# Loading the V weights and computing the first V product in column halves, the normalisations of later chunks one step sooner, and more filler before one double visit, in a fused attention and gated-MLP kernel

## The chip, the cores and the metric

The kernel runs on one core of one Trainium2 chip. The metric is device microseconds of one execution, given as a median of several runs. The profile's span is about 1.7 us shorter than the device time of the same run (263.7 against 265.41 us before the change).

Names used below: PE is TensorE's matmul row and PEld its weight loads, DVE is VectorE, ACT is ScalarE, POOL is GpSimd, SP the engine that issues the transfers. PSUM is the memory that matmuls write; this kernel uses eight banks of it.

## The reference

The result is `x + attention(norm(x)) + mlp(norm(x))` for 2048 rows of 512 columns in bf16:

```python
xn = _layernorm(x, axis=-1)
# attention: 32 heads of 16 columns, each query sees itself and the 255 keys before it
q, k, v = split(xn @ wqkv)
p = softmax(where(mask, q k^T / 4, -1e9));  a = (p @ v) @ wo
# MLP without a nonlinearity, F = 1792
m = ((xn @ w_gate) * (xn @ w_up)) @ w_down
return x + a + m
```

## The kernel before

The rows are handled in four chunks T of 512 (four blocks b of 128 rows each). The heart is a list of 75 *score steps*. A step computes a PSUM tile of scores (there is only one such tile, four banks), ACT takes its exponential, POOL and DVE mask it. Between steps PE is filled from a list of other matmuls ("fillers": gate, up, down, Q/K/V products), in amounts set by a small cost model on the host: `GAP` is the least amount of filler after a step and `SHIFT` moves filler between steps. After some steps the *value sums* of one group of heads (a single visit) or of two groups (a double visit) are computed.

```python
GAP = 9.6
PAIRS = ((0,), (1,), (2,), (3,)), ((0, 1), (2, 3)), ((0, 1), (2, 3)), ((0, 1), (2,))   # visits of each chunk
SHIFT = {20: -2, ..., 62: 3, 63: 6, 64: 8, 66: 8, 67: 6, 68: 4, 69: 2}

# loads, all from SP in this order
for lo, hi in ((0, 1), (1, 2), (2, 4)):                      # x, blocks 0, 1, 2-3
    nc.sync.dma_start(out=self.x[:, lo:hi, :], in_=xv[:, lo:hi, :])
for lo in (1024, 512, 0):                                    # V, K, Q weights, 512 KB each
    nc.sync.dma_start(out=self.Wqkv[:, :, lo:lo + 512], in_=wq[:, :, lo:lo + 512])
# ... cut: the other weights and the rest of x

# the first chunk: DVE normalises, PE transposes (ACT copies the transpose out), PE makes V
self.norm_transpose(0, False)
self.keep_busy(8)                                            # eight idle matmuls
for b in range(4):
    if b < 3:
        self.norm_transpose(b + 1, False)
    self.proj_v(b, engine="act" if b == 2 else "dve")
    if b == 0:
        self.norm_apply(3)
self.proj_qk(0, 0, 1, engine="dve")                          # K, then Q, then the first score step

# the normalisations of chunk T+1 run beside five score steps of chunk T
for i, fs in norms(T + 1, 0, 1).items():
    self.beside[self.first[T, 0] + (5, 6, 7, 8, 9)[i]] = fs

# a normalisation: DVE statistics, POOL scale (rs), then DVE applies it
nc.vector.tensor_scalar(out=xn[:], in0=self.x[:, t, :], scalar1=mv[:, j, 0:1],
                        scalar2=rs[:, j:j + 1], op0=ALU.subtract, op1=ALU.mult)

# a finished output block leaves its PSUM bank through DVE
nc.vector.tensor_tensor(out=y, in0=ps, in1=y, op=ALU.add)

# a visit of the value sums takes two PSUM banks for each group of heads
accs = [self.ps_m.tile([128, 512], F32, tag="M", name="acc") for _ in range(2)]
```

The softmax here doesn't subtract the row's maximum and nothing guards it: scores larger than these inputs give would overflow.

Of the kernel before, what the change touches and what calls it, by code (L numbers as in the profile page):

```python
# [22 lines left out]
REST = (((0, *SIX), (1, *SIX), (0, *FOUR)), ((1, *FOUR), (2, *FOUR)), ((2, *SIX), (3, *SIX), (3, *FOUR)))  # L23
SCORES, VALUES, SECOND = 1.9, 6.0, 5.0
FIRST = 3
GAP = 9.6
PAIRS = ((0,), (1,), (2,), (3,)), ((0, 1), (2, 3)), ((0, 1), (2, 3)), ((0, 1), (2,))
SHIFT = {20: -2, 21: -5, 22: -8, 23: -11, 24: -14, 26: -10, 27: -7, 28: -3, 62: 3, 63: 6, 64: 8, 66: 8, 67: 6, 68: 4, 69: 2}
MASKED, FIRST_DIVIDE, SECOND_DIVIDE = 8, 8, 24
COPY = dict(act=2.8, dve=3.2)  # L30
EXP, MASK, HALF, SUMS, DIVIDE, TURN, STATS = 8.7, 1.9, 1.7, 4.2, 8.2, 6.1, 4.2
# [2 lines left out]
class Kernel:  # L34
# [26 lines left out]
    def setup(self):  # L61
        nc, const, NT, NF = self.nc, self.const, self.NT, self.NF
        self.x = const.tile([128, NT, 512], BF16, name="x")
        self.Wqkv = const.tile([128, 4, 1536], BF16, name="Wqkv")
        self.Wo = const.tile([128, 4, 512], BF16, name="Wo")
        self.Wg = const.tile([128, 4, self.F], BF16, name="Wg")
        self.Wu = const.tile([128, 4, self.F], BF16, name="Wu")
        self.Wd = const.tile([128, NF, 512], BF16, name="Wd")
        xv = self.x_d.rearrange("(t p) d -> p t d", p=128)
        wq = self.w_d["qkv"].rearrange("(k p) n -> p k n", p=128)  # L70
        wg = self.w_d["g"].rearrange("(k p) n -> p k n", p=128)
        wu = self.w_d["u"].rearrange("(k p) n -> p k n", p=128)
        for lo, hi in ((0, 1), (1, 2), (2, 4)):
            nc.sync.dma_start(out=self.x[:, lo:hi, :], in_=xv[:, lo:hi, :])
        for lo in (1024, 512, 0):
            nc.sync.dma_start(out=self.Wqkv[:, :, lo:lo + 512], in_=wq[:, :, lo:lo + 512])
        h = self.F // 2
        for lo in (0, h):
            nc.sync.dma_start(out=self.Wg[:, :, lo:lo + h], in_=wg[:, :, lo:lo + h])
            nc.sync.dma_start(out=self.Wu[:, :, lo:lo + h], in_=wu[:, :, lo:lo + h])  # L80
            if lo == 0:
                nc.sync.dma_start(out=self.x[:, 4:8, :], in_=xv[:, 4:8, :])
        nc.sync.dma_start(out=self.Wd[:], in_=self.w_d["d"].rearrange("(f p) n -> p f n", p=128))
        wo = self.w_d["o"].rearrange("(c p) n -> p c n", p=128)
        for c in range(4):
            nc.sync.dma_start(out=self.Wo[:, c, :], in_=wo[:, c, :])
        for lo, hi in ((8, 10), (10, 12), (12, NT)):
            nc.sync.dma_start(out=self.x[:, lo:hi, :], in_=xv[:, lo:hi, :])

        warm = const.tile([128, 1], F32, name="warm")  # L90
        nc.vector.memset(warm[:], 0.0)
        nc.scalar.activation(out=warm[:], in_=warm[:], func=ACT.Exp)
        self.idle = const.tile([128, 128], BF16, name="idle")
        nc.vector.memset(self.idle[:], 0.0)
        self.keep_busy(40)
        ident = const.tile([128, 128], BF16, name="ident")
        nc.gpsimd.memset(ident[:], 0.0)
        nc.gpsimd.affine_select(out=ident[:], in_=ident[:], compare_op=ALU.not_equal, fill=1.0,
                                base=0, pattern=[[-1, 128]], channel_multiplier=1)
        self.ident = ident  # L100
        pi = const.tile([128, 1], I32, name="pi")
        nc.gpsimd.iota(pi[:], pattern=[[0, 1]], base=0, channel_multiplier=1)
        podd = const.tile([128, 1], I32, name="podd")
        nc.vector.tensor_scalar(out=podd[:], in0=pi[:], scalar1=4, scalar2=1,
                                op0=ALU.arith_shift_right, op1=ALU.bitwise_and)
        self.odd = const.tile([128, 1], F32, name="odd")
        nc.vector.tensor_copy(out=self.odd[:], in_=podd[:])
        self.mhalf = const.tile([128, 4], F32, name="mhalf")
        nc.gpsimd.memset(self.mhalf[:], -0.5)
        self.diag = const.tile([128, 64], BF16, name="diag")  # L110
        self.far = const.tile([128, 64], BF16, name="far")
        nc.gpsimd.memset(self.diag[:], BIG)
        nc.gpsimd.memset(self.far[:], BIG)
        for half in (slice(0, 64), slice(64, 128)):
            self.triangle(self.diag[half], True)
            self.triangle(self.far[half], False)
        self.xnT, self.Q, self.hT, self.OT = {}, {}, {}, {}
        self.K, self.Ko, self.V, self.VS = {}, {}, {}, {}
        self.strips, self.parts, self.at = {}, {}, {}
        self.stock = []  # L120
        self.new_values()
# [109 lines left out]
        else:  # L231
            nc.vector.tensor_copy(out=out, in_=in_)

    def proj_v(self, t, ks=range(4), engine=None):
        nc = self.nc
        T, b = divmod(t, 4)
        ps = self.bank(ks, "vp")
        for k in ks:
            nc.tensor.matmul(ps[:], lhsT=self.xnT[T][:, b, k, :],  # L239
                             rhs=self.Wqkv[:, k, 1024:1536], start=(k == 0), stop=(k == 3))  # L240
        if 3 not in ks:
            return
        self.copy(self.heads(self.V[T])[:, b].rearrange("p (r g) d -> p r g d", r=2)[:, :, :, 0:16],
                  ps.rearrange("p (g r d) -> p r g d", g=16, r=2), engine)
# [21 lines left out]
    def first_chunk(self):  # L266

        self.new_chunk(0)
        for b in range(2):
            self.norm_stats(b, 1)  # L270
            self.norm_scale(b, 1)
        for b in (0, 1, 2):
            self.norm_apply(b)
            if b < 2:
                self.norm_stats(b + 2, 1)
                self.norm_scale(b + 2, 1)
        self.norm_transpose(0, False)
        self.keep_busy(8)
        for b in range(4):
            if b < 3:  # L280
                self.norm_transpose(b + 1, False)
            self.proj_v(b, engine="act" if b == 2 else "dve")
            if b == 0:
                self.norm_apply(3)
        self.proj_qk(0, 0, 1, engine="dve")
        self.proj_qk(0, 0, 0, engine="act")
        self.swap_halves(0, self.nc.scalar)
        self.proj_qk(0, 1, 1, engine="dve")
# [160 lines left out]
    def fillers(self):  # L449


        out = []
# [21 lines left out]
        def gu(T, fs, between={}):  # L474
            for f in fs:
                for ks in halves:
                    add(2, lambda f=f, ks=ks: self.gate(T, f, ks))
                for ks in halves:
                    add(2, lambda f=f, ks=ks: self.up(T, f, ks))
                for g in between.get(f, ()):  # L480
                    add(*g)

        def norms(T, at, step):

            t, out = 4 * T, {}
            for b in range(4):
                for k, f in enumerate((lambda b=b: self.norm_stats(t + b, 1),
                                       lambda b=b: self.norm_scale(t + b, 1),
                                       lambda b=b: self.norm_apply(t + b),
                                       lambda b=b: self.norm_transpose(t + b, True))):  # L490
                    out.setdefault(at + step * b + (0, 0, 1, 1)[k], []).append((0, f))
            return out

        def down(T, b, part=range(0, NF, 2)):
            for lo in part:
                add(1.5 if (T, b) == (NCH - 1, 3) else 2, lambda lo=lo: self.down(T, b, lo, lo + 2))

        def wo(T, b, cs):
            add(len(cs), lambda: self.wo(T, b, cs), None, self.last[T, cs[-1]])
# [4 lines left out]
        for T in range(NCH):  # L504
            if T:
                if T + 1 < NCH:
                    for i, fs in norms(T + 1, 0, 1).items():
                        self.beside[self.first[T, 0] + (5, 6, 7, 8, 9)[i]] = fs
                gu(T, range(FIRST))
                for b in range(4):  # L510
                    down(T - 1, b)
                    wo(T - 1, b, range(4))
                    add(0, lambda T=T, b=b: self.store(T - 1, b))
                gu(T, range(FIRST, NF))
            else:
                gu(T, range(NF), norms(1, 1, 3))
            if T + 1 < NCH:
                project(T + 1)
        T = NCH - 1
# [6 lines left out]
    def run(self):  # L526
# [47 lines left out]
        for g, s in enumerate(steps):  # L574
# [8 lines left out]
            self.scores(*s)  # L583
            upto = max(total * (g + 1) / len(steps) + SHIFT.get(g, 0), spent + GAP)
            if g in (1, 2):
# [80 lines left out]
```

## Time and profile before

| | before |
|---|---|
| device time, median of the first 3 runs | 265.57 us |
| span of the profile | 263.7 us |
| PE busy | 98% |
| first score step starts | 13.53 us |
| the five double visits | 2.56, 2.40, 2.60, 2.40, 2.57 us |

From the page of the kernel before: the span, the busy time of the engines, and the engines on the chain that ended last.

```profile
span 263.7 us, 8896 instructions
...
PE 259.6 (98%) x3890; PEld 120.3 (46%) x3890; DVE 174.2 (66%) x341; ACT 175.9 (67%) x142; POOL 117.3 (44%) x278
...
PE 97%; DVE 1%; DMA 1%; issue 0%
```

The list of waits of PE (engine, line, what it waited for, us in total, times, longest) names only the start:

```profile
PE wps L127 <- DVE idle L94: 1.1, 1, 1.1
PE xTp L209 <- DVE xn L190: 0.3, 1, 0.3
```

The chain that ended last lists the value sums with start and length. These are the five double visits of the kernel before:

```profile
89.78 2.56 PE acc L366 x190
...
124.48 2.40 PE acc L366 x175
...
155.57 2.60 PE acc L366 x162
...
187.72 2.40 PE acc L366 x175
...
221.40 2.57 PE acc L366 x177
```

The start, as PE saw it (start, length, engine, line, operation; in brackets the idle time before and what ended it; wps are idle matmuls, xTp transposes, vp V products, S scores):

```profile
5.14 0.40 PE L209 MATMUL xTp<-ident,xn 128*128 128x128 bf16 x4
5.37 0.61 PE L127 MATMUL wps<-idle 128*128 128x128 bf16 x8
6.32 0.40 PE L209 MATMUL xTp<-ident,xn 128*128 128x128 bf16 x4 [0.34 <-DVE xn L190]
6.75 1.02 PE L239 MATMUL vp<-Wqkv,xnT 128*128 128x512 bf16 x4
...
9.12 1.89 PE L239 MATMUL vp<-Wqkv,xnT 128*128 128x512 bf16 x8
...
13.53 0.28 PE L312 MATMUL S<-Q,K 16*64 16x192 bf16 x4
```

The V weights were complete at 6.62 us (the last of the 16 completion records of that transfer), so the first V product at 6.75 could not have come much sooner.

### The profile page before, as it was taken

What the parts mean: (1) busy time and instruction counts of PE and PEld (TensorE: products, weight loads), DVE (VectorE), ACT (ScalarE), POOL (GpSimd) and SP (SyncE); (2) the same over time, 40 slices, a digit from 0 to 9 for tenths busy, and PEclk for the clock granted to TensorE, in tenths of its full rate; (3) what the DMA queues carried; (4) which work ended last, traced back from release to release, by engine and by line L of the source; (5) the groups of instructions that cost most, each with busy time, mean ns of one, the idle gap of its engine ahead of it and who ended that gap; (6) DMA issues with size and microseconds to landing.
All of it is one profiled execution on the core that took longest, in us unless ns stands there. A gap on an engine that the chain in (4) does not pass through costs nothing.

```text
span 263.7 us, 8896 instructions
## 1 busy us (share of the span) xinstructions
PE 259.6 (98%) x3890; PEld 120.3 (46%) x3890; DVE 174.2 (66%) x341; ACT 175.9 (67%) x142; POOL 117.3 (44%) x278
## 2 busy tenths in 40 slices
PE   7999999999999999999999999999999999999995
PEld 7444444444444544444544454444544445444453
DVE  6677888777726697557963679766685235887244
ACT  3467688888757776677775567767777546887500
POOL 6225343325447744333455654544453452554600
PEclk9999999999999999999999999999999999999999
DMA  6999911220002710002000320001100100000002
GB/s 206 374 354 341 268 21 22 24 47 4 0 22 54 69 24 0 4 0 47 5 0 22 81 65 2 0 2 24 27 4 0 42 21 25 2 0 2 4 2 80
DMA packets 19431, 15.12 MB, mean 57 GB/s; under 512 B 7360, under 2 KB 19392, under 8 KB 19392
## 3 DMA queue, kind: packets, MB, share of 16 engines
q1 hardware_dynamic: 18848, 14.26, 20.3%
q8 instruction: 30, 0.49, 0.8%
q10 hardware_dynamic: 544, 0.30, 0.4%
q14 instruction: 9, 0.07, 0.1%
HBM read 9.70 MB, written 2.10 MB: 45 GB/s over the span
## 4 chain that ended last, share of the span: by engine, by line
PE 97%; DVE 1%; DMA 1%; issue 0%
PE gp L395 19%; PE up L406 19%; PE psd L428 17%; PE qkp L251 11%; PE S L312 10%; PE acc L366 7%; PE vp L239 5%; PE psd L434 5%; PE L L428 2%; DMA x<-in_A_x_dram 1%; DVE st L169 1%; PE L L434 1%; PE L L366 0%; PE xTp L209 0%; DVE xn L190 0%; DVE mv L170 0%
## 5 line engine op out<-in xcount | busy, mean ns | idle before, releaser
L319 ACT ACTIVATE P<-S 128x2048 bf16<-128x2048 f32 x75 | 140.7, 1876 | 51.5 <-PE S L312 44.6
L158 POOL TENSOR_SCALAR_AFFINE_SELECT P<-P 64x256 bf16<-64x256 bf16 x224 | 101.3, 452 | 126.0 <-ACT P L319 111.6
L395 PE MATMUL gp<-xnT,Wg 128*128 128x512 bf16 x224 | 60.2, 380 | 0.0
L406 PE MATMUL up<-xnT,Wu 128*128 128x512 bf16 x224 | 58.8, 380 | 0.0
L411 DVE TENSOR_TENSOR hT<-up,gsb 128x512 bf16<-128x512 f32 x56 | 38.3, 684 | 18.6 <-PE up L406 11.6
L428 PE MATMUL psd<-Wd,hT 128*128 128x512 bf16 (+1 forms) x210 | 48.0, 369 | 0.0
L343 DVE TENSOR_TENSOR P<-P,diag 128x512 bf16<-128x512 bf16 (+1 forms) x75 | 29.1, 388 | 9.5 <-ACT P L319 9.5
L428 PEld LDWEIGHTS <-hT 128*128 128x128 bf16 x238 | 21.3, 98 | 25.1 <-issue 2.9
L406 PEld LDWEIGHTS <-Wu 128*128 128x128 bf16 x224 | 20.6, 98 | 25.6 <-issue 2.3
L395 PEld LDWEIGHTS <-Wg 128*128 128x128 bf16 x224 | 20.1, 98 | 24.9 <-issue 2.1
L312 PE MATMUL S<-Q,K 16*64 16x320 bf16 (+4 forms) x720 | 31.0, 260 | 0.0
L312 PE MATMUL S<-Q,Ko 32*64 32x320 bf16 (+4 forms) x720 | 31.0, 260 | 0.0
L251 PE MATMUL qkp<-xnT,Wqkv 128*128 128x512 bf16 x128 | 29.9, 380 | 0.0
L230 ACT ACTIVATE gsb<-gp 128x512 bf16<-128x512 f32 x40 | 23.5, 596 | 7.5 <-PE gp L395 6.7
L312 PEld LDWEIGHTS <-K 16*64 16x64 bf16 x720 | 12.1, 103 | 30.7 <-issue 30.7
L372 DVE STREAM_TRANSPOSE at<-acc 128x512 f32<-128x512 f32 x30 | 19.3, 690 | 6.8 <-PE acc L366 6.8
L444 DVE TENSOR_TENSOR x<-psd,x 128x512 bf16<-128x512 f32 (+1 forms) x15 | 9.7, 653 | 16.4 <-PE psd L434 16.4
L251 PEld LDWEIGHTS <-Wqkv 128*128 128x128 bf16 x128 | 11.7, 98 | 14.5 <-issue 1.6
L366 PE MATMUL acc<-P,V 64*32 64x320 bf16 (+4 forms) x672 | 18.0, 253 | 0.0
L366 PE MATMUL acc<-P,VS 64*32 64x320 bf16 (+4 forms) x672 | 18.0, 253 | 0.0
L366 PEld LDWEIGHTS <-V 64*32 64x32 bf16 x720 | 15.0, 91 | 2.4 <-issue 2.0
L239 PE MATMUL vp<-Wqkv,xnT 128*128 128x512 bf16 x64 | 15.3, 380 | 0.0
(54 smaller groups left out, 198.2 us busy)
## 6 DMA issues: line engine op xcount, KB each, us to landing
out_dram<-x SPq DMA_DIRECT2D x15, 128.0 KB, 1.7
Wg<-in_B_w_gate_dram SPq DMA_DIRECT2D x2, 896.0 KB, 10.9
Wu<-in_B_w_up_dram SPq DMA_DIRECT2D x2, 896.0 KB, 12.5
Wd<-in_B_w_down_dram SPq DMA_DIRECT2D x1, 1792.0 KB, 17.6
Wqkv<-in_A_wqkv_dram SPq DMA_DIRECT2D x3, 512.0 KB, 5.4
x<-in_A_x_dram SPq DMA_DIRECT2D x2, 512.0 KB, 8.3
VS<-V SPq DMA_DIRECT2D x6, 144.0 KB, 2.6
x<-in_A_x_dram SPq DMA_DIRECT2D x3, 256.0 KB, 7.1
```

Of the source, the lines that this page charges most:

```text
L158: nc.gpsimd.affine_select(out=v, in_=v, pattern=pattern + [[1 if diag else -1, 64]], compare_op=ALU.is_ge if diag else ALU.is_gt, fill=0.0 ...
L230: nc.scalar.activation(out=out, in_=in_, func=ACT.Copy)
L239: nc.tensor.matmul(ps[:], lhsT=self.xnT[T][:, b, k, :], rhs=self.Wqkv[:, k, 1024:1536], start=(k == 0), stop=(k == 3))
L251: nc.tensor.matmul(ps[:], lhsT=self.Wqkv[:, k, lo:lo + 128], rhs=self.xnT[T][:, :, k, :], start=(k == 0), stop=(k == 3))
L312: nc.tensor.matmul(S[64 * par:64 * par + 64, e, col:col + n], lhsT=(self.Ko if par else self.K)[U, c][rows, keys], rhs=self.Q[T, c][rows, ...
L319: nc.scalar.activation(out=P[:, :, 0:col], in_=S[:, :, 0:col], func=ACT.Exp, scale=0.25)
L343: self.nc.vector.tensor_tensor(out=v, in0=v, op=ALU.min, in1=self.diag.unsqueeze(1).unsqueeze(1).to_broadcast([128, 4, n, 64]))
L366: nc.tensor.matmul(accs[par][32 * e:32 * e + 32, q:q + n], lhsT=v, rhs=P[rows, e, col:col + n], start=(i == 0), stop=(i == len(todo) - 1), ...
L395: nc.tensor.matmul(ps[:], lhsT=self.Wg[:, k, 128 * f:128 * f + 128], rhs=self.xnT[T][:, :, k, :], start=(k == 0), stop=(k == 3))
L406: nc.tensor.matmul(ps[:], lhsT=self.Wu[:, k, 128 * f:128 * f + 128], rhs=self.xnT[T][:, :, k, :], start=(k == 0), stop=(k == 3))
L411: nc.vector.tensor_tensor(out=self.hT[T, f][:], in0=ps[:], in1=self.gsb[:], op=ALU.mult)
L428: nc.tensor.matmul(ps, lhsT=self.hT[T, f][:, 128 * b:128 * b + 128], rhs=self.Wd[:, f, c0:c1], start=(f == 0), stop=False)
```

## The change

Four edits with one intent, to take small waits of PE away: V weights in two column halves so that half of the first V product can fill the wait at 6.0 us; the second half after the transposes of block 1; the normalisations of later chunks one score step sooner; and more filler before the fifth double visit (`GAP`, `SHIFT`). The late loads of x are merged from three to two.

```diff
-GAP = 9.6
+GAP = 10.6
-SHIFT = {..., 62: 3, 63: 6, 64: 8, 66: 8, 67: 6, 68: 4, 69: 2}
+SHIFT = {..., 62: 3, 63: 6, 64: 12, 66: 12, 67: 11, 68: 9, 69: 6, 70: 3}
-        for lo in (1024, 512, 0):
-            nc.sync.dma_start(out=self.Wqkv[:, :, lo:lo + 512], in_=wq[:, :, lo:lo + 512])
+        for lo, hi in ((1024, 1280), (1280, 1536), (512, 1024), (0, 512)):
+            nc.sync.dma_start(out=self.Wqkv[:, :, lo:hi], in_=wq[:, :, lo:hi])
-        for lo, hi in ((8, 10), (10, 12), (12, NT)):
+        for lo, hi in ((8, 12), (12, NT)):
# cut: proj_v takes cols=(lo, hi), multiplies those columns, and copies out when hi is 512
-        self.keep_busy(8)
-        for b in range(4):
-            if b < 3:
-                self.norm_transpose(b + 1, False)
-            self.proj_v(b, engine="act" if b == 2 else "dve")
-            if b == 0:
-                self.norm_apply(3)
+        self.keep_busy(4)
+        self.proj_v(0, cols=(0, 256))
+        first = self.cur
+        self.norm_transpose(1, False)
+        self.cur = first
+        self.proj_v(0, engine="act", cols=(256, 512))
+        self.norm_apply(3)
+        self.proj_v(1, (0, 1))
+        self.norm_transpose(2, False)
+        self.proj_v(1, (2, 3), engine="dve")
+        self.norm_transpose(3, False)
+        self.proj_v(2, engine="act")
+        self.proj_v(3, engine="dve")
-                        self.beside[self.first[T, 0] + (5, 6, 7, 8, 9)[i]] = fs
+                        self.beside[self.first[T, 0] + (4, 5, 6, 7, 8)[i]] = fs
```

In PE's order the start differs as written; of the steps, only 64 to 72 differ (22 matmuls instead of 18 before the fifth double visit, then +2, -2, -2, -2).

More of the change, by code (lines that the diff above doesn't have):

```diff
@@ L25 @@
 FIRST = 3
-GAP = 9.6
+GAP = 10.6
 PAIRS = ((0,), (1,), (2,), (3,)), ((0, 1), (2, 3)), ((0, 1), (2, 3)), ((0, 1), (2,))
-SHIFT = {20: -2, 21: -5, 22: -8, 23: -11, 24: -14, 26: -10, 27: -7, 28: -3, 62: 3, 63: 6, 64: 8, 66: 8, 67: 6, 68: 4, 69: 2}
+SHIFT = {20: -2, 21: -5, 22: -8, 23: -11, 24: -14, 26: -10, 27: -7, 28: -3, 62: 3, 63: 6, 64: 12, 66: 12, 67: 11, 68: 9, 69: 6, 70: 3}
 MASKED, FIRST_DIVIDE, SECOND_DIVIDE = 8, 8, 24
@@ L232, in copy, with proj_v @@
             nc.vector.tensor_copy(out=out, in_=in_)
-    def proj_v(self, t, ks=range(4), engine=None):
+    def proj_v(self, t, ks=range(4), engine=None, cols=(0, 512)):
         nc = self.nc
         T, b = divmod(t, 4)
-        ps = self.bank(ks, "vp")
+        lo, hi = cols
+        ps = self.bank(ks if lo == 0 else (), "vp")
         for k in ks:
-            nc.tensor.matmul(ps[:], lhsT=self.xnT[T][:, b, k, :],
-                             rhs=self.Wqkv[:, k, 1024:1536], start=(k == 0), stop=(k == 3))
-        if 3 not in ks:
+            nc.tensor.matmul(ps[:, lo:hi], lhsT=self.xnT[T][:, b, k, :],
+                             rhs=self.Wqkv[:, k, 1024 + lo:1024 + hi], start=(k == 0), stop=(k == 3))
+        if 3 not in ks or hi < 512:
             return
```

## The prediction

> **What bounds the kernel now.** TensorE (PE). The page gives PE 98% busy; the chain that ended last is 97% PE, and the waits show PE idle only twice: 1.1 us before its first matmul and 0.3 us at 6.0 us (for the second normalised block). From 13.5 us on, PE's timeline is one packed sequence: a score step costs about 0.36 us, a 512-column matmul 0.215 us, a double visit of the value sums 2.40 to 2.60 us, wherever they stand. Reordering after 13.5 us cannot shorten that sum. Slack is left only in the start (V products end at 11.0 us), about 0.04 us in the third double visit (2.60 us against its siblings' 2.56), and the tail of stores, which is not touched.
>
> **What the change does, costed.**
> 1. Start. Four idle matmuls (0.06 us each) go; the first V product becomes 4+4 matmuls of 256 columns (0.87 us in all, as before), one half before and one after the transposes of block 1. Old timeline: block-0 transposes 5.14, xnT copies on ACT 5.46 to 6.12, V weights landed 6.62 (DMA completions), second xn 6.26, V products from 6.75 to 11.0. New: half the V weights should land near 6.0 (estimate: 512 B packets at about 27 ns, between 18 ns for 256 B and 36 ns for 768 B). Half product 6.05 to 6.5, transposes of block 1 at 6.5 (0.2 us LATER than before, as PE is in order), other half 6.9 to 7.3, V(1) from 7.55 when its 0.60 us ACT copy is done, transposes of block 2 at 8.0, of block 3 at 8.7 (before 8.88: no DVE copy stands before xn(3) now), V(2) at 9.1, V(3) ends near 10.8. Gain about 0.2 us; nothing if the half weights land 0.25 us later; best case 0.35.
> 2. Norms a step sooner: DVE and DMA work off the critical path, at most 0.04 us.
> 3. GAP and SHIFT: the built order differs only in steps 64 to 72: 22 matmuls instead of 18 before the fifth double visit, then +2, -2, -2, -2. The sum is unchanged: no gain. Steps 69 to 72 become about 2.62 us long. There is one score tile: a step lasts at least the 0.50 us until exp starts plus its 1.88 us, about 2.45 us (estimate from these); ten-matmul steps of 2.62 us ran before without a stall.
> 4. V weights in two transfers: K weights land about 0.25 us later than 8.1 us, Q at about 9.9; both are needed after 10.8.
>
> The Trainium skill, "TensorE: Matmul & The Clock Gate", section "What's actually happening", says the array runs at half clock until it was busy for a window of about 3.4 us. The trace agrees: the clock turns full at 4.69 us, 3.6 us after the first idle matmul. Fewer idle matmuls after that do not bring it back; the gaps stay under 0.5 us.
>
> **Prediction.** 265.57 to about 265.38 us; 8 in 10 between 264.95 and 265.70. Faster by over 2%: 0.01; within 2%: 0.98; slower by over 2%: 0.01.
>
> **What would show it.** Start: first Q/K matmul at about 10.8 us instead of 11.0, first score at 13.3 instead of 13.53, every later score shifted alike until step 64. Step 3: no new PE wait between steps 64 and 73, the tail from the last value visit still 11.5 us. Wrong: transposes of block 1 after 6.7 us, or PE waiting for ACT before V(1) and V(2) for over 0.4 us in all.
>
> **What would make it wrong.** Slower 512 B packets; a PSUM or ACT stall in steps 69 to 72 (up to 0.5 us slower); a larger gain if the first half lands before the xnT copies.

## More of the kernel before

A double visit needs all four remaining PSUM banks at once.

The waits of PEld in a window around the first double visit (89 to 93 us), cut to the line that matters:

```profile
PEld L366 <- DVE x L444: 0.2, 1, 0.2
```

DVE around the first visit (start, length, engine, line, operation; in brackets the idle time before and what ended it):

```profile
88.19 0.39 DVE L343 TENSOR_TENSOR P<-P,diag 128x512 bf16<-128x512 bf16 x1
89.85 0.48 DVE L190 TENSOR_SCALAR xn<-x,mv,rs 128x512 bf16<-128x512 bf16 x1 [1.27 <-POOL rs L182]
90.25 0.67 DVE L444 TENSOR_TENSOR x<-psd,x 128x512 bf16<-128x512 f32 x1
```

DVE stood idle for 1.27 us until POOL delivered `rs` for a normalisation, and only then did it take the next instruction in its order, which empties the PSUM bank `psd`. That ended at 90.92 us. The visit began at 89.70, and its third bank was that one: the first weight load of the second group of heads is recorded at 90.982 us, 0.20 us after the instruction before it. The wait of the third visit stands earlier, before the ninth instruction of the visit (155.73 us), and the trace puts it down to another DVE instruction that follows the same kind of normalisation: the copy of a gate product (L232), which also empties a PSUM bank.

## The result

The changed kernel took 265.14 us (median of 6 runs, 264.93 to 265.49) against 265.46 us (6 runs, 265.25 to 265.64). The ratio is 0.9991 with a 95% interval of 0.9978 to 1.0003. A ratio here is the mean time of one kernel's fast runs over that of the other's of the same rounds, so it is not quite the ratio of the medians. Two later sets of the same kernel gave 0.9976 (0.9964 to 0.9988) and 0.9975 (0.9962 to 0.9988). So it is faster by 0.2 to 0.7 us, far inside 2%.

The profile of the changed kernel has the same span as before, 263.7 us (its run, 265.40 us, was one of the slower of the six), but not for want of differences. Two large ones cancel. First, the five double visits, again from the chain that ended last:

```profile
90.28 2.40 PE acc L373 x175
...
124.82 2.40 PE acc L373 x175
...
155.91 2.40 PE acc L373 x175
...
187.86 2.40 PE acc L373 x175
...
222.41 2.40 PE acc L373 x175
```

All five take 2.40 us now; 0.16, 0.20 and 0.17 us are gone. DVE around the first of them:

```profile
87.47 0.48 DVE L190 TENSOR_SCALAR xn<-x,mv,rs 128x512 bf16<-128x512 bf16 x1 [1.27 <-POOL rs L182]
87.88 0.41 DVE L350 TENSOR_TENSOR P<-P,diag 128x512 bf16<-128x512 bf16 x1
89.09 0.69 DVE L451 TENSOR_TENSOR x<-psd,x 128x512 bf16<-128x512 f32 x1 [0.81 <-PE psd L441]
```

The same wait of 1.27 us for POOL is still there, but a step earlier, and the bank is emptied at 89.78 us, as soon as PE has finished with it and before the visit begins at 90.20.

Second, the start. The waits of PE:

```profile
PE wps L127 <- DVE idle L94: 1.1, 1, 1.1
PE vp L240 <- DMA Wqkv<-in_A_wqkv_dram: 0.7, 1, 0.7
```

and its timeline:

```profile
5.36 0.40 PE L209 MATMUL xTp<-ident,xn 128*128 128x128 bf16 x4
5.59 0.39 PE L127 MATMUL wps<-idle 128*128 128x128 bf16 x4
6.12 0.67 PE L240 MATMUL vp<-Wqkv,xnT 128*128 128x256 bf16 x4
6.62 0.39 PE L209 MATMUL xTp<-ident,xn 128*128 128x128 bf16 x4
7.66 1.03 PE L240 MATMUL vp<-Wqkv,xnT 128*128 128x256 bf16 x6 [0.65 <-DMA Wqkv<-in_A_wqkv_dram]
...
9.61 1.90 PE L240 MATMUL vp<-Wqkv,xnT 128*128 128x512 bf16 x8
...
14.03 0.28 PE L319 MATMUL S<-Q,K 16*64 16x192 bf16 x4
```

The first half product filled the gap as intended (6.12 us), but the second half of the weights was complete only at 7.62 us, a whole microsecond after the old single transfer. PE waited 0.65 us for it, and the first score step came at 14.03 us instead of 13.53.

So the first profile suggested a theory that is not the predicted one. **Theory B**: the gain comes from the double visits, mostly through the sooner normalisations, and the new start costs time. The rivals: **theory A**, the prediction (start gains, the rest is nothing), and **chance**: the late weights, or the wait in the fifth visit, are accidents of one execution.

### The profile page after: what moved, and what is told of

The parts are those of the page before. It is cut to its first block, busy times and chain, and to the rows that moved or that the text cites. A ratio compares the mean times of both kernels' runs of the same rounds, so it can differ in the third digit from the quotient of the medians.

```text
span 263.7 us, 8896 instructions
## 1 busy us (share of the span) xinstructions
PE 259.1 (98%) x3890; PEld 120.7 (46%) x3890; DVE 174.7 (66%) x341; ACT 176.1 (67%) x142; POOL 116.9 (44%) x278
## 4 chain that ended last, share of the span: by engine, by line
PE 96%; DMA 2%; SPq 1%; issue 0%; DVE 0%
PE gp L402 19%; PE up L413 19%; PE psd L435 17%; PE qkp L252 11%; PE S L319 10%; PE acc L373 6%; PE vp L240 5%; PE psd L441 5%; PE L L435 2%; DMA Wqkv<-in_A_wqkv_dram 2%; PE L L441 1%; PE L L373 0%; SPq L74 0%; SPq L76 0%; PE xTp L209 0%
## 5 line engine op out<-in xcount | busy, mean ns | idle before, releaser
L230 ACT ACTIVATE gsb<-gp 128x512 bf16<-128x512 f32 x39 | 22.9, 596 | 8.2 <-PE gp L402 7.4
L240 PE MATMUL vp<-Wqkv,xnT 128*128 128x512 bf16 (+1 forms) x68 | 15.6, 367 | 0.8 <-DMA Wqkv<-in_A_wqkv_dram 0.7
```

What stands on the lines that cost most here:

```text
L230: nc.scalar.activation(out=out, in_=in_, func=ACT.Copy)
L240: nc.tensor.matmul(ps[:, lo:hi], lhsT=self.xnT[T][:, b, k, :], rhs=self.Wqkv[:, k, 1024 + lo:1024 + hi], start=(k == 0), stop=(k == 3))
```

## The experiments

Twelve runs were made, four in each of three sets (two of them repeat the changed kernel unaltered, one repeats e4_old_start); the kernels of a set ran on one chip beside the kernel before. All gave correct results. "Visits" are the lengths of the double visits from start to start in PE's timeline; "first score" is the start of the first score step.

| run | what it is | median us | ratio to before (95%) | first score | visits 1, 3, 5 |
|---|---|---|---|---|---|
| before (first profile) | | 265.46 to 265.69 | 1 | 13.53 | 2.56, 2.60, 2.57 |
| e1_norms | norms only | 265.12 | 0.9980 (0.9966 to 0.9993) | 13.35 | 2.40, 2.40, 2.81 |
| e2_shift | GAP, SHIFT only | 265.64 | 1.0000 (0.9988 to 1.0013) | 13.59 | 2.82, 2.80, 2.40 |
| e3_start | start only | 265.92 | 1.0010 (0.9998 to 1.0023) | 13.94 | 2.83, 2.79, 2.40 |
| e4_old_start | all but the start | 264.83 | 0.9969 (0.9957 to 0.9982) | 13.42 | 2.40, 2.40, 2.40 |
| after_again | changed kernel | 264.88 | 0.9976 (0.9964 to 0.9988) | 13.73 | 2.40, 2.40, 2.40 |
| e5_halves_in_order_only | changed, V weights whole | 265.55 | 0.9999 (0.9987 to 1.0011) | 13.84 | 2.40, 2.40, 2.40 |
| e6_halves_in_load_only | e4, V weights in halves | 265.21 | 0.9993 (0.9973 to 1.0014) | 14.69 | 2.40, 2.40, 2.40 |
| e7_stream_place | e1, four idle matmuls fewer | 265.66 | 1.0001 (0.9989 to 1.0013) | 13.87 | 2.40, 2.40, 2.42 |
| e8_k_halves | e4, V weights in row halves | 265.29 | 0.9979 (0.9967 to 0.9992) | 14.67 | 2.40, 2.40, 2.40 |
| e9_old_start_again | e4 repeated | 265.04 | 0.9970 (0.9958 to 0.9982) | 13.48 | 2.40, 2.40, 2.40 |
| after_third | changed kernel | 265.04 | 0.9975 (0.9962 to 0.9988) | 13.72 | 2.40, 2.40, 2.40 |
| e10_old_shift | changed, old GAP, SHIFT | 265.22 | 0.9979 (0.9967 to 0.9991) | 13.85 | 2.40, 2.40, 2.40 |

The two columns on the right account for nearly everything. Take from each profile's span the start of the first score step and what the double visits took over 2.40 us: 249.62 to 249.76 us are left in thirteen of the fourteen profiles (249.64 before, 249.66 after). The fourteenth, e5, has 250.26, with a wait of 0.5 us told below. So little room is left for any other effect of the change on the profiled executions, the merged late loads of x included, which no run tests alone.

### Each part alone, and all but the start

**e1_norms**, the kernel before with one line changed:

```diff
-self.beside[self.first[T, 0] + (5, 6, 7, 8, 9)[i]] = fs
+self.beside[self.first[T, 0] + (4, 5, 6, 7, 8)[i]] = fs
```

> Kernel before with only the norms a step sooner. Theory A (as predicted): they are off the critical path, at most 0.04 us faster. Theory B (from the two traces): in the first and third double visit TensorE waits 0.16 and 0.20 us for a PSUM bank that VectorE still empties, because the normalisation stands ahead of that work in VectorE's order; a step sooner it is out of the way, so both visits take 2.40 us instead of 2.56 and 2.60, and the time falls by about 0.36 us. The fifth visit stays at 2.57 us. The first score step stays near 13.5 us.

Measured: ratio 0.9980; by the means of the set, 265.14 against 265.66, so 0.52 us faster. The first and third visit fell to 2.40 us. Theory A allowed 0.04 us and falls. The fifth visit was unchanged in kind, and longer in this run: 2.81 us. The chain shows the fifth torn in two, and the waits of PEld in that window (220 to 224 us) name no engine. From the chain:

```profile
89.59 2.40 PE acc L366 x175
...
155.22 2.40 PE acc L366 x174
...
220.85 1.67 PE acc L366 x121
222.64 1.02 PE acc L366 x55
```

and from the waits:

```profile
PEld L366 <- issue: 0.4, 1, 0.4
```

**e2_shift**, only `GAP` and `SHIFT`:

```diff
-GAP = 9.6
+GAP = 10.6
-SHIFT = {..., 64: 8, 66: 8, 67: 6, 68: 4, 69: 2}
+SHIFT = {..., 64: 12, 66: 12, 67: 11, 68: 9, 69: 6, 70: 3}
```

> Kernel before with only GAP and SHIFT changed. Theory A: the sum of TensorE's work is the same, no change. Theory B: the fifth double visit goes from 2.57 to 2.40 us and the time falls by about 0.17 us; the first and third visit stay at 2.56 and 2.60. Rival C: the gap inside the fifth visit names no semaphore in the trace, so it may be a chance event of one execution; then the fifth visit may be 2.40 us also in the other runs, and this kernel is as fast as before.

Measured: ratio 1.0000. The fifth visit was 2.40 us, as theory B said; but the first and third were 2.82 and 2.80 us, longer than in the first profile of before. The size of the wait in visits 1 and 3 is thus not fixed: 0.16 to 0.20 us in one profile, 0.39 to 0.42 in two others (this one and e3_start's). In this run the normalisation that DVE waited for began at 90.17 us with the visit at 89.77, in the first profile at 89.85 with the visit at 89.70, so DVE was 0.25 us later against PE. That is consistent with the 0.52 us that the norms alone gave, more than the 0.36 us taken from the first profile.

**e3_start**, only the first chunk and the loads (the diff of the change without its `GAP`, `SHIFT` and norm lines):

> Kernel before with only the new start (V weights in halves, first V product in halves, x in two late loads instead of three). Theory A: 0.2 us faster, first score step at 13.3 us. Theory B: the profile of the changed kernel had its first score at 14.03 us, 0.50 later, since the second half of the V weights landed at 7.62 us; so this kernel is 0 to 0.5 us slower. Rival C: that late landing was a chance of one execution, and on the mean of the runs the start gains 0.1 to 0.2 us.

Measured: ratio 1.0010 (0.9998 to 1.0023), 0.30 us slower by the means of the set, just short of clear. The second half of the V weights was complete at 7.54 us and the first score came at 13.94. The predicted gain of 0.2 us is not there; the sign is against it. The waits of PEld around the first visit (89 to 93 us) show the old wait at its larger size:

```profile
PEld L373 <- DVE x L451: 0.5, 1, 0.5
```

and here the wait of the third visit is long enough to show in the waits of PE:

```profile
PE acc L373 <- DVE gsb L232: 0.2, 1, 0.2
```

**e4_old_start**, the changed kernel with the old first chunk and loads put back:

> The changed kernel with the old start put back (norms sooner, GAP and SHIFT as changed). Theory A: 0 to 0.04 us faster than before. Theory B: all three visits at 2.40 us, about 0.5 us faster than before, first score at 13.5 us, faster than the changed kernel by what its start costs. Rival C: about 0.35 us faster than before and a little slower than the changed kernel.

Measured: ratio 0.9969, 0.79 us faster by the means (264.88 against 265.66), all visits at 2.40 us. This is what theory B expected, with a larger size.

### What of the new start costs

**after_again**, the changed kernel, unaltered:

> The changed kernel unaltered, for a second profile and as the control of this set. If the late second half of the V weights (7.62 us in its first profile, 7.54 in the run of the start alone) is a property of the new start, it lands after 7.4 us again and the first score stands at 13.9 us or later; if it was chance, it lands near 6.9 us and the first score near 13.4. Double visits 2.40 us each.

Measured: 264.88 us, ratio 0.9976. The second half of the V weights was complete at 7.17 us and the first score came at 13.73: between the two expectations. Late weights are a property of the new start; how late varies.

**e5_halves_in_order_only**, the changed kernel with the V weights in one transfer:

```diff
-for lo, hi in ((1024, 1280), (1280, 1536), (512, 1024), (0, 512)):
+for lo, hi in ((1024, 1536), (512, 1024), (0, 512)):
```

> The changed kernel with the V weights loaded in one transfer again; the product of block 0 stays in halves around the transposes. Theory D (the split transfer is what hurts): V weights land at 6.5 us as in the old start, and the first score comes earlier than in the changed kernel, at 13.8 us or before. Theory E (the order is what hurts): since TensorE is in order, transposes of block 1 now wait for the weights (about 7.0 us instead of 6.3), and the first score stays at about 13.9 us, 0.4 later than with the old start.

Measured: 265.55 us, ratio 0.9999, so 0.6 us slower than the changed kernel of its set. The weights were complete at 6.25 us, sooner than in any other run, and yet the first score came at 13.84; PE's waits at the start are 0.5 us for weights, 0.5 us for the normalised block and 0.3 us for ACT. This run also had one wait of 0.5 us of a score step on the exponential, after the start, so not all of its loss belongs to the order. The first score lies between what the two theories said (13.8 and 13.9). But the transposes of block 1 started at 6.82 us instead of 6.32, after the wait for the weights, as theory E said: the new order does not pay unless the weights come in halves, and with them whole it is no better.

**e6_halves_in_load_only**, the old order with the V weights in halves (edit in e4_old_start):

```diff
-for lo in (1024, 512, 0):
-    nc.sync.dma_start(out=self.Wqkv[:, :, lo:lo + 512], in_=wq[:, :, lo:lo + 512])
+for lo, hi in ((1024, 1280), (1280, 1536), (512, 1024), (0, 512)):
+    nc.sync.dma_start(out=self.Wqkv[:, :, lo:hi], in_=wq[:, :, lo:hi])
```

> The kernel of the run with the old start (norms sooner, GAP and SHIFT as changed), with only the V weight transfer cut in two. Theory D: the second half lands near 7.5 us instead of 6.5, the first V product starts then, and the first score comes at 14.0 us or later, 0.5 us slower than with the old start. Theory E: the transfer is harmless, first score at 13.5 us, total as with the old start.

Measured: first score at 14.69 us, the second half complete at 7.79 us, as theory D expected, and PE waits a whole microsecond for it. The waits of PE:

```profile
PE vp L239 <- DMA Wqkv<-in_A_wqkv_dram: 1.0, 1, 1.0
```

The times are spread (264.84 to 266.77 us), median 265.21, so the profiled execution (266.19) was a bad one, and the mean cost is smaller than that profile shows. In this profile the transfer hurts. By the times its cost is not clear: this set has no run of e4_old_start, and the two intervals overlap (0.9973 to 1.0014 here, 0.9957 to 0.9982 there).

**e8_k_halves**, an attempt at a better version: V weights halved by rows, so that packets stay at 1 KB, and the first product halved the same way (edit in e4_old_start):

```diff
-for lo in (1024, 512, 0):
+for k0 in (0, 2):
+    nc.sync.dma_start(out=self.Wqkv[:, k0:k0 + 2, 1024:1536], in_=wq[:, k0:k0 + 2, 1024:1536])
+for lo in (512, 0):
 # cut
-for b in range(4):
+self.proj_v(0, (0, 1))
+self.norm_transpose(1, False)
+self.proj_v(0, (2, 3), engine="dve")
+self.norm_apply(3)
+for b in (1, 2, 3):
```

> A version meant to beat both: the kernel with the old start (norms sooner, GAP and SHIFT as changed), with the V weights loaded in two halves by rows (contraction blocks 0-1, then 2-3), so packets stay at 1 KB, and the first V product in two such halves, one before and one after the transposes of block 1. Eight idle matmuls are kept, so TensorE's instruction stream keeps its length. If the cost of the new start lies in its 512 B packets, V weights are complete near 6.6 us, and the first score comes at 13.1 to 13.4 us, 0.1 to 0.3 us faster than with the old start. If any cut of that transfer costs, the second half lands after 7.3 us and the first score is at 13.8 us or later.

Measured: a miss. The second half was complete at 8.28 us, the first score came at 14.67, and the kernel (265.29 us) was not faster than the one with the old start (265.04 us). The waits of PE:

```profile
PE vp L241 <- DMA Wqkv<-in_A_wqkv_dram: 1.4, 1, 1.4
```

So the load came late without the small packets too. In every run with the V load cut in two, by columns or by rows, its last byte came between 7.1 and 8.3 us; in every run with it whole, between 6.25 and 6.95. Why a cut transfer completes later was not found. The packets themselves were, by the median, as fast as estimated (27 ns for 512 B, 46 ns for 1 KB). But between 5 and 7 us the seven profiles with a cut load moved 173 to 306 GB/s, and the seven with a whole one 290 to 369. Also, SP issued the second half 0.5 us after the first (2.70 against 2.18 us in the changed kernel's first profile); no run separates that from the cut itself.

**e9_old_start_again** and **after_third**, the two side by side in one set:

> The kernel with the old start, repeated as control beside the changed kernel on one chip. If the new start costs what the single-change run showed (0.25 us), this is about 0.2 us faster than the changed kernel; if the start is neutral, the two are the same. First score near 13.5 us, all double visits 2.40 us.

> The changed kernel unaltered, third profile. First score between 13.7 and 14.0 us as in its first two profiles, double visits 2.40 us, 0.3 to 0.7 us faster than before.

Measured: medians of 265.04 us for both; by the means, 264.99 with the old start and 265.11 with the new. First scores at 13.48 and 13.72 us. The profiles put the new start later in every one of five (13.72 to 14.03, against 13.35 to 13.59 in five with the old start; 0.38 us on the mean; e7's 13.87 is told below). The times say 0.30 us slower alone (interval touching zero) and 0.13 us, undecided, in this pair. It gains nothing; its cost is a few tenths at most.

### The fifth visit

The wait in the fifth visit names no semaphore. In the trace of before and of e1_norms it stands before the same instruction, number 6593 of PE's recorded instructions (7787 in all). The page shows a queue of kind "instruction" with 30 transfers and 0.49 MB, so 16 KB each; 7787 over 30 is about 260 instructions for each.

The Trainium skill says why that may matter ("Runtime: NRT & Kernel Launch", section "Instruction fetch mechanics"): an engine's instructions come in blocks of 16 KiB, which are 256 instructions, fetched while the current ones execute. If the wait is for such a block, it can only stand at block boundaries.

**e7_stream_place** is e1_norms with four idle matmuls fewer, eight instructions:

```diff
-self.keep_busy(8)
+self.keep_busy(4)
```

> Norms sooner alone, with four idle matmuls fewer before block 1 (they fill a wait, so no time is expected from that). In two profiles of kernels with the old SHIFT the fifth double visit stalled (0.16 and 0.41 us) at the same place of TensorE's instruction stream with no semaphore, in one it did not. Theory F (the stall hangs on the place in the stream, which this edit moves by 8 instructions, as the new SHIFT did): fifth visit at 2.40 us, 0.2 to 0.3 us faster than the run with only the norms. Theory G (chance, or the spacing of the steps): it may stall again, total as the run with only the norms, about 0.5 us faster than before.

Measured: 265.66 us, not faster but 0.5 us slower than e1_norms was against its own set. The fifth visit was 2.42 us, but now the fourth double visit was torn. From the chain:

```profile
187.69 1.67 PE acc L366 x122
189.57 1.02 PE acc L366 x55
```

and from the waits of PEld (187 to 191 us):

```profile
PEld L366 <- issue: 0.5, 1, 0.5
```

It stands before instruction 5569. The distance to 6593 is 1024, which is four times 256. So the three unexplained waits (0.16, 0.41 and 0.50 us) all stand at the same place modulo 256, as a wait for an instruction block would. In a double visit PE takes an instruction about every 6 ns (2.40 us for 384 instructions), so a block is used up in 1.6 us, where elsewhere it lasts some 10 us. The transfer before each of these waits started 2.2 to 2.9 us ahead of the wait's end. The part of theory F that said the stall would vanish was wrong: it moved. The loss of time is not all from it, since in the profiled execution x arrived late (its third transfer at 5.46 us, 4.4 to 5.2 us in the others) and delayed the start to 13.87 us.

The kept traces say more. Count a block from each such place (193, 449, 705 and so on), and pair the start of the second block with the first transfer of the instruction queue, the third with the second, and so on: 406 starts in the fourteen profiles. Ordered by the time from the end of the transfer to the start of the block, the three waits (1.23, 1.40 and 1.50 us) are among the first five; the next start comes at 1.60 us. So PE waited where a block had only just arrived. The other two of the five are number 6593 in e7 (1.27 us, hardly a wait: 0.02 us) and in e3_start (1.43 us, none).

**e10_old_shift**, the changed kernel with the old `GAP` and `SHIFT`:

> The changed kernel with the old GAP and SHIFT (only start and norms changed). Theory F (instruction blocks): the fifth double visit can stall again at instruction 6593 of TensorE's stream by up to 0.4 us, since only 18 matmuls stand between the previous step and the visit, so this is 0 to 0.4 us slower than the changed kernel, by 0.2 on the mean. Theory A (SHIFT does nothing): same time as the changed kernel, visit at 2.40 us.

Measured: 265.22 us against 265.04 of the changed kernel in the set (means 265.21 and 265.11), visit five at 2.40 us: undecided, and no stall in this profile. In all, the fifth visit waited over 0.1 us in 2 of 5 profiles with the old `SHIFT`, and in none of 9 with the new one. Number 6593 came 1.27 to 1.63 us after the end of its transfer in those 5, and 1.74 to 2.49 us in the 9. That fits: the four matmuls that the new `SHIFT` adds before the visit stand in the block that ends there, so the transfer has more time. In pairs of one set, the new `SHIFT` gained 0.27 us on top of the norms (e1_norms to e4_old_start), 0.10 us in the changed kernel, and nothing in the kernel before. That it helps is likely, by 0 to 0.3 us from one execution to the next; a gain in time is not shown.

### What was not tried

No run takes the instruction fetch away, or moves it alone, so that cause rests on the place and the timing of the waits: it is argued, not shown. Why the cut load is late is open. Combinations of the new order with earlier weights, for instance V weights ahead of the third x block, were not built.

## Why the prediction was right or wrong

The number was right: 265.38 us was forecast, 265.14 measured, inside the range of 264.95 to 265.70. The reasons behind it were not, so this was luck.

- **Step 1, the start: wrong in sign.** "Gain about 0.2 us" rested on a second half of the weights available when PE got to it at 6.9 us. The packets did take the estimated 27 ns, and the first half was there (5.4 to 5.9 us). But the second half was complete at 7.1 to 7.6 us. Alone, the new start measured 0.30 us slower, not clear of noise, and gained nothing in any run. The condition was stated ("nothing if the half weights land 0.25 us later"), but for the wrong half.
- **Step 2, the norms: wrong by a factor of over ten.** "At most 0.04 us" came from comparing the third double visit (2.60 us) with "its siblings' 2.56". The right sibling was the visit of 2.40 us, named in the same paragraph: the work is identical. The wait was hidden because only PE's own list of waits was read; it stood in the weight loads' list, as a wait on DVE. Measured: 0.52 us from this line alone.
- **Step 3, GAP and SHIFT: right by the time measured, wrong in reasoning.** Alone they changed nothing. But that the stretches cost the same "wherever they stand" does not hold: the fifth visit took 2.40 to 2.81 us in kernels where nothing but its place and the execution differed.
- **Step 4, later K and Q weights:** never waited for, right; but they landed at 10.10 and 11.57 us in the first profile, where about 8.35 and 9.9 us were forecast.
- **The clock:** The Trainium skill ("TensorE: Matmul & The Clock Gate", section "What's actually happening") was used rightly. Fewer idle matmuls did not bring back the slow clock: by the pace of the first matmuls it was full from about 4.7 us before and 5.2 us after, and the changed kernel ran its 256-column products at full speed in its first profile. The agreement in the moment (3.6 us after the first idle matmul) was one case, though: with the same forty idle matmuls the pace turned full 2.6 us after the first in e5 and about 5 us after it in e9. In e10 the first half product still ran partly slow (its matmuls 188 and 213 ns apart, 108 ns at full pace).

A gain that was not predicted and a loss that was predicted as a gain cancelled to within the noise of the first profile. Without the single-change runs the forecast would have looked confirmed.

The fastest kernel is the changed one without its new start: 0.9969 and 0.9970 of the time before in two sets. Against the changed kernel itself it is 0.13 us ahead in the mean, which these runs cannot tell from zero.

## What to carry to other kernels

Where stretches of identical work differ in length, the shortest is the floor and every other one holds a wait; look for it in the weight loads' waits too, since the matmul row counted as busy during such waits here. An in-order helper engine that waits for one thing holds up everything behind it, so put work that waits (a normalisation) well ahead of work that frees a buffer the critical engine is about to need. Before cutting a load to use its first part sooner, measure when its last part arrives.

## What the Trainium skill lacked or had wrong

- "Runtime: NRT & Kernel Launch", section "Instruction fetch mechanics", says that crossing a block boundary is mostly hidden. Three waits without a semaphore stood at places that agree with its 256-instruction blocks (5569, and 6593 twice), of 0.50, 0.16 and 0.41 us, in stretches where PE took 384 instructions in 2.40 us. The page explains the hiding by an issue floor of about 20 cycles for an instruction; it does not say how long a block takes to arrive. Here the waits ended 1.2 to 1.5 us after the end of the transfer.
- "DMA: Bandwidth & Descriptors", section "Specifications", gives 512 B as the least transfer for line rate. Packets of 512 B took 27 ns and packets of 1 KB 46 ns here, so by estimate 303 against 356 GB/s over 16 engines (512 x 16 / 27 and 1024 x 16 / 46): packets of 512 B were 15% below packets of 1 KB.
- "Perfetto Trace Analysis", section "DMA Optimizations", says that splitting a transfer may let a part start sooner, and the whole end sooner when the DMA engines are mostly idle. Here they were not idle (DMA busy share 0.84 to 1.08 between 5 and 7 us), and no page says how much later the last part can arrive. A 512 KB load was complete at 6.25 to 6.95 us whole, and at 7.1 to 8.3 us in halves, with packets of 512 B or of 1 KB alike.
